# Value products in blocks of four from the first head on, and seven later query products spread over the feed-forward groups

## The chip, the cores and the metric

The kernel runs on one core of a Trainium2 chip. The metric is the device time of one execution in microseconds (us), smaller is better; three runs of the kernel before have a median of 1342.93 us (1341.37 to 1343.72). The profiled execution, whose trace is read here, took 1341.01 us, of which 1338.9 us lie between its first and its last instruction (the span). Differences of under 0.2% (2.7 us) are what a measurement of this kernel cannot tell from no change.

## The reference

With x of 2048 rows and 512 columns, in float32:

```python
q = (x @ wq) in 32 heads of 16; k = x @ wk; v = x @ wv      # one key and value head for all
p = softmax(q k^T / 4);  a = (p @ v, heads side by side) @ wo
b = (silu(x @ w_gate) * (x @ w_up)) @ w_down                # 1792 wide inside
g = sigmoid(sum(x * gate_w));  out = g * a + (1 - g) * b
```

Each head has 2048 x 2048 scores, so exp is taken of 134 million numbers in all.

## The kernel before, in words

Every product outside the value product is made of split operands: a number is a high part (fp32r) and a low part, and three products (high high, high low, low high) are summed. TensorE (PE) is shared by two kinds of work that are woven into one stream by hand (`manual_schedule`: each engine's instructions stand in the order in which the Python code makes them).

**Attention.** A unit u is one head (u // 16) and one block of 128 keys (u % 16). `score(u, j)` (line 669) makes one tile: 128 keys against 1024 queries, two matmuls that each use 64 rows of the array. ScalarE (ACT) takes exp of the tile, from PSUM (two tiles `pss`) to the SBUF tile `pt` (line 684); in some cases VectorE (DVE) first copies half of a tile to SBUF (line 680) and ACT takes exp of that half there. `mix(u)` (line 688) multiplies the exps of a unit with the values and a column of ones, four matmuls in groups of 32 array columns, summed into the PSUM tile `po` over the 16 units of a head. At a head's end `po` is copied to `osb`, inverted, multiplied and stored in DRAM (`o_d`), in small pieces that are handed out over the next units (`LATER`).

**Fillers.** The list `JOBS` holds query products (`query(m, c)`: heads 8m to 8m+7, 512 of the rows), gate and up products of the feed-forward part (`gate_up`) and down products (`down`). A job has 12 or 15 steps; `Halves.step` (line 401) makes one step of one job on the lower 64 rows of the array and one of an older job on the upper 64 rows, side by side. The scores and the fillers use the array in 64-row halves; `mix` uses it in 32-column groups. The gate and up weights of the next columns are loaded by SyncE's (SP's) queue into a raw tile (`wraw`, two buffers) and split on GpSimd (POOL) into a high and a low tile (line 135); `load_w` is called for the first nine weights after the line that loads head 1's queries (lines 781 to 786).

**The order before.** After the keys and values, the four query products of m = 0 run, and three more of m = 1 (`fill(GAP)`, line 648). Then come 16 rounds of two units each (`BEGIN`, lines 790 to 811): four score tiles, eight filler steps, `settle` (what DVE still owes the fillers), and `mix` of two units. In these rounds the other nine query products are the first fillers, and only then the first gate product. One transitional block (`TURN`, line 817) follows, and then blocks of four units (line 821): eight score tiles and 16 filler steps in the order `STEPS`, DVE's half copies for three of eight tiles (`KINDS`), and `mix` of four units in one go. After the last unit the jobs that are left run whole, and then the output product.

**Query products before.** The end of a query product (`keep`, line 224) for m > 0 is five DVE instructions (high part, low part, scaled, absolute bound, largest value) and three stores to DRAM (`q_d`), from which `load_head` fetches each head's queries one head ahead.

Of the kernel before, what the change touches and what calls it, by code (L numbers as in the profile page):

```python
# [46 lines left out]
PTB = 3  # L47
WRB = 2
BLOCK = 4
BEGIN = 16  # L50
STOP = 2
EARLY = 6
OUTS = (1, 2, 3, 0)
# [3 lines left out]
TURN = "SS" + "SFF" * 8  # L57
# [5 lines left out]
def tile_gated_mix(ctx, tc, x, wq, wk, wv, wo, w_gate, w_up, w_down, gate_w, out):  # L63
# [30 lines left out]

    qpool = tc.alloc_tile_pool(name="qpool", bufs=1, side="right")
# [7 lines left out]
    ACC, PAIR = {}, []  # L103
# [19 lines left out]
    ACTS, DEFER, LOADS, HOLD, EVAC, FRESH = [], [], [], [], [], set()  # L123
# [5 lines left out]
    def settle():  # L129
        FRESH.clear()  # L130
        run(ACTS, len(ACTS))
        while DEFER:
            DEFER.pop(0)[2]()
# [77 lines left out]
    def load_wq(m):  # L211
        WQ[m] = load_split(wq_v[:, :, m * P:(m + 1) * P], f"wq{m}", 1, qpool)

    def query(m, c):
# [8 lines left out]

        def keep(ps):
            qh = wp.tile([P, CH], F32R, name="hh", bufs=7)
            ql = wp.tile([P, CH], F32R, name="hl", bufs=7)

            if m:
                qb = wp.tile([P, CH], F32, name="ht" if c % 2 else "hs", bufs=2)
                nc.vector.tensor_copy(qh, ps)  # L230
            else:
                qb = wp.tile([P, CH], F32R, name="hl" if c % 2 else "hh", bufs=7).bitcast(F32)
                nc.scalar.activation(qh, ps, AF.Copy)
                nc.scalar.activation(qb.bitcast(F32R), ps, AF.Abs, scale=kmax)
            nc.vector.tensor_tensor(ql, ps, qh.bitcast(F32), ALU.subtract)
            if m:
                nc.vector.tensor_scalar(qb, qh.bitcast(F32), kmax, None, op0=ALU.mult)
                nc.vector.scalar_tensor_tensor(qb.bitcast(F32R), qb, -1.0, qb, op0=ALU.mult, op1=ALU.max)
# [7 lines left out]
            def store():  # L246
                for j, part in enumerate(parts):
                    nc.sync.dma_start(q_d[m * HG:(m + 1) * HG, j * DH:(j + 1) * DH, cs], part.bitcast(F32))

            if m:  # L250
                store()
            else:
                STORES.append(store)
            nc.vector.tensor_reduce(top[:, t:t + 1], qb, axis=AX.X, op=ALU.max)

        return Job(3 * KD, lambda: m in WQ, terms, keep)

    def queries():
        jobs = [query(m, c) for m in range(1, KD) for c in range(NCH)]
        jobs[-1].after.append(open_acc)  # L260
        jobs[-1].after.append(lambda: nc.vector.tensor_reduce(top[:, KD * NCH:], top[:, :KD * NCH], axis=AX.X, op=ALU.max))
        return jobs

    def open_acc():
        qpool.release()
        for name in ("accp", "bp2"):
            PAIR.append(tc.alloc_tile_pool(name=name, bufs=3, side="right"))
# [60 lines left out]
    def down(ns, c, i):  # L328
# [11 lines left out]
        def add(ps):  # L340
            if c not in ACC:
                ACC[c] = PAIR[0].tile([P, TC, D], F32, name="acc")
# [11 lines left out]


    def jobs():
        late = []
        for m, c in enumerate(ORDER):
            for fs in GROUPS:
# [137 lines left out]
    with tc.tile_pool(name="apool", bufs=1) as ap, tc.tile_pool(name="apool2", bufs=2) as a2:  # L497
# [71 lines left out]
        def project_kv(c):  # L569
            cs = slice(c * CH, (c + 1) * CH)  # L570
            if c % 2 == 0:
                VZ[c // 2] = ap.tile([KW, 2 * CH], F32, name="vz", bufs=2)
# [33 lines left out]
        with tc.manual_schedule():  # L606
# [28 lines left out]
            for c in range(NCH):  # L635
# [5 lines left out]
                if c == 0:  # L641
# [6 lines left out]
            fill(GAP)  # L648

# [3 lines left out]
    with tc.tile_pool(name="bpool", bufs=2) as bp:  # L653
# [11 lines left out]
        def new_pt(u):  # L665
            late = u > PTB * (BEGIN * 2 // PTB) and (u - 2 * BEGIN) % (2 * PTB) >= PTB
            PT[u] = (PAIR[1] if late else bp).tile([P, S], F32, name="pt", bufs=PTB)

        def score(u, j, half=False):
            h, kt = divmod(u, NT)  # L670
            if j == 0:
                new_pt(u)
# [54 lines left out]
        def block(k, first, last, steps, kinds, order):  # L727
# [48 lines left out]
            FRESH.clear()  # L776
            for u in range(BLOCK * k, BLOCK * (k + 1)):
# [9 lines left out]
        with tc.manual_schedule():  # L787
            for j in range(2):
                exps(*score(0, j))
            for n in range(BEGIN):  # L790
                quota = RATE
                u = 2 * n
                if n == 0:
                    feed(FIRST)
                exps(*score(u + 1, 0))
                if n == 0:
                    feed(quota - FIRST)
                exps(*score(u + 1, 1))
                feed(FIRST)
                exps(*score(u + 2, 0))  # L800
                feed(quota - FIRST)
                exps(*score(u + 2, 1))
                settle()
                mix(u)
                mix(u + 1)
                halves.clock += LONG
                run(COPY, 1)
                if LATER:
                    LATER.pop(0)[1]()
                if n == NT // 2 + 1:  # L810
                    load_head(2)
            assert PAIR
            for k in range(2 * BEGIN // BLOCK, NB):
                u = BLOCK * k
                if k == 2 * BEGIN // BLOCK:
                    n = u + 6 - (u + 1)
                    block(k, u + 1, u + 6, TURN, "A" * 2 * n, [f"{i}d" for i in range(2 * n)])
                elif k == NB - 1:
# [13 lines left out]
    PAIR.pop().release()  # L832

    with tc.tile_pool(name="tpool", bufs=2) as tp, tc.tile_pool(name="rpool", bufs=1, side="right") as rp, \
# [3 lines left out]
        ACC[0] = rp.tile([P, TC, D], F32, name="again")  # L838

# [7 lines left out]
        while JOBS:  # L847
            assert JOBS[0].ready()

            if len(JOBS) == TC:  # L850
# [16 lines left out]
    PAIR.pop().release()  # L867
# [78 lines left out]
```

## Time and profile before

| what | value |
|---|---|
| median of three runs | 1342.93 us |
| profiled execution | 1341.01 us, span 1338.9 us |
| PE busy | 1327.0 us (99%) |
| ACT busy | 1061.6 us (79%) |
| DVE busy | 710.1 us (53%) |
| POOL busy | 226.1 us (17%) |
| first score tile starts | 47.94 us |
| first `mix` of the block after the transitional one | 146.87 us |
| `mix` of the last full block | 1251.87 us |

Times in the views are counted from the first instruction. A row of the timeline has start, length, engine, line, operation, `out<-in`, the shape in the array (`64*128` is a half of the rows, `128*32` a group of columns), and in brackets the idle time before it and what ended it. SPq is SP's queue of transfer issues; POOL rows are a little rough. A row of the windows has a stretch and its length, and then the busy time of each engine (with the number of instructions), PEclk, the share in which the transfer engines were busy and what they moved.

### The profile page before, as it was taken

The numbers are of one execution on the slowest core, as the hardware profiler recorded it, in microseconds if no ns is written. First come the engines' busy times: TensorE is split into PE (matmuls) and PEld (weight loads), VectorE is DVE, ScalarE is ACT, GpSimd is POOL, SyncE is SP. The second block draws the span as 40 slices with busy tenths as digits, with TensorE's granted clock in tenths as the row PEclk, the third lists the DMA queues.
The fourth block names the chain that finished last, engine by engine and source line by source line (L and its number), as shares of the span: only waits on it lengthen the run. The fifth ranks groups of instructions, "written<-read, shape, count | busy, mean of one in ns | idle before, by whom it ended". The sixth has DMA issues, their size and how long they took to land. (4 is left out here: it accounts for less than half of the span.)

```text
span 1338.9 us, 26760 instructions
## 1 busy us (share of the span) xinstructions
PE 1327.0 (99%) x10743; PEld 768.8 (57%) x10743; DVE 710.1 (53%) x1221; ACT 1061.6 (79%) x1463; POOL 226.1 (17%) x240
## 2 busy tenths in 40 slices
PE   9999999999999999999999999999999999999998
PEld 7655555555555555555555555555555555555586
DVE  4555565565456565555555556455445555455442
ACT  4578888888888888888888888888888888888500
POOL 6140321152042141143020000000000000001234
PEclk9999999999999999999999999999999999999999
DMA  8455221141234372265162442242122442333254
GB/s 278 139 182 184 66 60 37 36 107 45 59 108 147 121 230 68 68 216 155 46 212 71 135 122 84 68 144 85 56 95 68 134 139 68 99 116 107 63 174 143
DMA packets 104176, 151.83 MB, mean 113 GB/s; under 512 B 12656, under 2 KB 43632, under 8 KB 102384
## 3 DMA queue, kind: packets, MB, share of 16 engines
q1 hardware_dynamic: 102320, 149.86, 36.2%
q8 instruction: 88, 1.44, 0.5%
q10 hardware_dynamic: 1728, 0.20, 0.1%
q14 instruction: 40, 0.33, 0.1%
HBM read 98.11 MB, written 51.38 MB: 112 GB/s over the span
## 5 line engine op out<-in xcount | busy, mean ns | idle before, releaser
L684 ACT ACTIVATE pt<-pss 128x1024 f32<-128x1024 f32 (+1 forms) x1024 | 842.0, 876 | 177.1 <-PE pss L676 145.8
L680 DVE COPY pt<-pss 128x512 f32<-128x512 f32 x354 | 244.9, 692 | 420.9 <-PE pss L676 386.9
L696 PE MATMUL po<-pt,vaug 128*32 128x512 f32 x4096 | 467.6, 595 | 0.0
L676 PE MATMUL pss<-qs,ks 64*128 64x512 f32 x2048 | 402.7, 417 | 1.2 <-ACT pt L684 1.1
L676 PEld LDWEIGHTS pss<-qs,ks 64*128 64x128 f32 x2048 | 193.0, 184 | 219.1 <-ACT pt L684 183.4
L696 PEld LDWEIGHTS po<-pt,vaug 128*32 128x32 f32 x4096 | 119.2, 109 | 260.2 <-issue 255.2
L684 ACT ACTIVATE pt<-pt 128x512 f32<-128x512 f32 x354 | 195.7, 620 | 0.0
L192 PE MATMUL pf<-xh,wgl 64*128 64x512 f32 (+1 forms) x440 | 162.0, 391 | 0.0
L192 PE MATMUL pf<-xh,wgh 64*128 64x512 f32 (+1 forms) x440 | 160.5, 391 | 0.3
L192 PE MATMUL pf<-xl,wgh 64*128 64x512 f32 (+1 forms) x440 | 160.0, 390 | 0.0
L192 PE MATMUL pf<-xh,wuh 64*128 64x512 f32 (+1 forms) x440 | 158.3, 392 | 0.5 <-DVE sign L419 0.3
L192 PE MATMUL pf<-xl,wuh 64*128 64x512 f32 (+1 forms) x440 | 158.3, 390 | 0.0
L192 PE MATMUL pf<-xh,wul 64*128 64x512 f32 (+1 forms) x440 | 157.2, 391 | 0.2 <-POOL wul L108 0.2
L192 PE MATMUL pf<-wdh,hl 64*128 64x512 f32 (+1 forms) x427 | 143.8, 390 | 0.0
L192 PE MATMUL pf<-wdh,hh 64*128 64x512 f32 (+1 forms) x427 | 143.6, 390 | 0.0
L192 PE MATMUL pf<-wdl,hh 64*128 64x512 f32 (+1 forms) x427 | 143.4, 390 | 0.0
L705 DVE RECIPROCAL rsb<-rsb 128x128 f32<-128x128 f32 x128 | 117.1, 935 | 10.0 <-issue 7.8
L107 POOL CAST xh<-wraw 128x512 fp32r<-128x512 f32 x16 | 9.8, 611 | 555.8 <-DMA wraw<-o_d 555.8
L192 PEld LDWEIGHTS pf<-xh,wgh 64*128 64x128 f32 (+1 forms) x440 | 78.5, 185 | 9.1 <-issue 1.8
L192 PEld LDWEIGHTS pf<-xh,wuh 64*128 64x128 f32 (+1 forms) x440 | 77.2, 185 | 9.5 <-issue 1.9
L192 PEld LDWEIGHTS pf<-xl,wgh 64*128 64x128 f32 (+1 forms) x440 | 78.5, 185 | 5.5
L192 PEld LDWEIGHTS pf<-xh,wgl 64*128 64x128 f32 (+1 forms) x440 | 78.5, 185 | 5.3
(157 smaller groups left out, 1351.6 us busy)
## 6 DMA issues: line engine op xcount, KB each, us to landing
qs<-q_d SPq DMA_DIRECT2D x62, 192.0 KB
wraw<-in_B_w_gate_dram SPq DMA_DIRECT2D x28, 256.0 KB
wraw<-in_B_w_up_dram SPq DMA_DIRECT2D x28, 256.0 KB
wraw<-in_B_w_down_dram SPq DMA_DIRECT2D x28, 256.0 KB
wgh<-w_d SPq DMA_DIRECT2D x28, 256.0 KB
wgl<-w_d SPq DMA_DIRECT2D x28, 256.0 KB
wuh<-w_d SPq DMA_DIRECT2D x28, 256.0 KB
wul<-w_d SPq DMA_DIRECT2D x28, 256.0 KB
```

What stands on the lines that cost most here:

```text
L107: eng_hi.tensor_copy(hi, src)
L192: ins = nc.tensor.matmul(self.ps, a, b, start=(i == 0 and not half), stop=(last and half != 0))
L676: nc.tensor.matmul(ps[:, b * CH:(b + 1) * CH], ks[rows, kt * P:(kt + 1) * P], QS[h][rows, j, :], start=True, stop=True)
L680: other = nc.vector.tensor_copy(pt[:, CH:], ps[:, CH:]) if half else None
L684: ins = nc.scalar.activation(pt[:, w], ps[:, w], AF.Exp, scale=SCALE)
L696: nc.tensor.matmul(po[c * 2 * DH:(c + 1) * 2 * DH, :], vaug[:, kt, :], pt[:, c * CH:(c + 1) * CH], start=(kt == 0), stop=(kt == NT - 1))
L705: nc.vector.reciprocal(rsb[:, w], rsb[:, w])
```

## The change

It does four things at once.

1. The rounds of two units and the transitional block go. After an opening of four score tiles and eight filler steps (`OPEN`), all 128 blocks are of four units, with DVE's half copies and `mix` of four units. The six `pt` buffers come from one pool.
2. Of the twelve query products of m = 1 to 3, three run before the first score tile: (1, 2), (1, 3), (2, 3), those that read the upper half of x, which leaves SBUF there. Two, (1, 0) and (1, 1), are the first fillers. The other seven stand one each in the first seven feed-forward groups, after the group's fifth job (`LATE`).
3. A query product's high part, and its bound, are made by ACT for the three early ones (two instructions, as for m = 0). For the other nine DVE makes the high and the low part at once, and scaling, bound and largest value are put off (`DEFER`, or `SOON`, a block later). The seven late ones write to a tile of their own (`qh`) and to one of the two buffers of `osb`.
4. The split query weights, and the raw values `vz`, stand in the three accumulator tiles (`HOME`) until these are needed. `load_wq(3)` comes ahead of the stores of m = 0.

The core of the diff:

```diff
-PTB = 3
+PTB = 6
-BEGIN = 16
+EARLY_Q = ((1, 2), (1, 3), (2, 3))
+SECOND_Q = ((1, 0), (1, 1))
+LATE = {(0, 0): (2, 0), (0, 1): (3, 0), (0, 2): (2, 1), (1, 0): (3, 1), (1, 1): (2, 2), (1, 2): (3, 2), (2, 0): (3, 3)}
-TURN = "SS" + "SFF" * 8
+OPEN = "SFSFFFSFFFSF"
...
+        late = (m, c) in LATE.values()
+        behind = late or (m, c) in SECOND_Q
         def keep(ps):
...
+            if late:
+                qh = hp.tile([P, CH], F32R, name="qh", bufs=1)
+                ql = hp.tile([P, CH], F32, name="osb").bitcast(F32R)
+                qb = qh.bitcast(F32)
...
+            if behind:
                 nc.vector.tensor_copy(qh, ps)
             else:
                 nc.scalar.activation(qh, ps, AF.Copy)
                 nc.scalar.activation(qb.bitcast(F32R), ps, AF.Abs, scale=kmax)
             nc.vector.tensor_tensor(ql, ps, qh.bitcast(F32), ALU.subtract)
...
+            if behind:
+                store([0, 1])
+                (SOON if late else DEFER).extend([((m, c), 0.5, scale), ((m, c), 0.7, bound), ((m, c), 0.7, most)])
...
     def queries():
+        return [query(m, c) for m, c in EARLY_Q + SECOND_Q]
...
                     yield job
                     if late and j:
                         yield late.pop(0)
+                    if j == 4:
+                        if (m, GROUPS.index(fs)) in last:
+                            yield last[m, GROUPS.index(fs)]
...
+            load_wq(3)
             run(STORES, NCH)
-            load_wq(3)
             fill(GAP)
...
         with tc.manual_schedule():
-            for j in range(2):
-                exps(*score(0, j))
-            for n in range(BEGIN):
...
-            for k in range(2 * BEGIN // BLOCK, NB):
+            tiles = [(u, j) for u in range(2) for j in range(2)]
+            for what in OPEN:
+                if what == "S":
+                    exps(*score(*tiles.pop(0)))
+                else:
+                    feed(1)
+            for k in range(NB):
```

How the instructions stand now, at three places. First PE, right after the first value products (`pss` is a score tile, `pf` a filler's PSUM tile; line numbers of the two kernels differ). Before, two score tiles are followed by steps of two query products:

```order
L676 MATMUL pss<-qs,ks 128x512 [waits Activation_49]
L676 MATMUL pss<-qs,ks 128x512
L192 MATMUL pf<-xl,wq2h 128x512
L192 MATMUL pf<-xh_326,wq1h 128x512 [waits DVE_49]
L192 MATMUL pf<-xh,wq2l 128x512
L192 MATMUL pf<-xl_327,wq1h 128x512
```

Now the first gate product begins there, in the 25th filler step (`acc` is a query weight in its new home, `wgh` and `wgl` are the split gate weight):

```order
L704 MATMUL pss<-qs,ks 128x512 [waits Activation_49]
L704 MATMUL pss<-qs,ks 128x512
L198 MATMUL pf<-xh,wgh 128x512 [waits Pool_49]
L198 MATMUL pf<-xl,acc 128x512
L198 MATMUL pf<-xl,wgh 128x512
L198 MATMUL pf<-xh,acc 128x512
L198 MATMUL pf<-xh,wgl 128x512 [waits Pool_49]
```

The first gate product moved from the 109th filler step that PE takes after the first score tile to the 25th, and it waits for POOL's two split halves.

Second SP's queue, where the first gate weight is fetched. Before:

```order
L248 DMA q_d<-hh 8x16x512 [waits DMAHW0_49]
L248 DMA q_d<-hs 8x16x512 [waits DMAHW1_49,DVE_49]
L661 DMA qs<-q_d 16x2x512 [waits DMAHW2_49]
L662 DMA qs<-q_d 48x2x512 [waits DMAHW3_49]
L661 DMA qs<-q_d 16x2x512 [waits DMAHW4_49]
L662 DMA qs<-q_d 48x2x512 [waits DMAHW5_49]
L138 DMA wraw<-in_B_w_gate_dram 128x4x128 [waits DMAHW6_49,Pool_49]
L138 DMA wraw<-in_B_w_up_dram 128x4x128 [waits DMAHW7_49,Pool_49]
```

Now:

```order
L264 DMA q_d<-hh 8x16x512 [waits DMAHW0_49,Activation_49]
L264 DMA q_d<-ht 8x16x512 [waits DMAHW1_49,Activation_49]
L693 DMA qs<-q_d 16x2x512 [waits DMAHW2_49]
L694 DMA qs<-q_d 48x2x512 [waits DMAHW3_49]
L693 DMA qs<-q_d 16x2x512 [waits DMAHW4_49]
L694 DMA qs<-q_d 48x2x512 [waits DMAHW5_49]
L144 DMA wraw<-in_B_w_gate_dram 128x4x128 [waits DMAHW6_49,Pool_49]
L144 DMA wraw<-in_B_w_up_dram 128x4x128 [waits DMAHW7_49,Pool_49]
```

The first gate weight keeps its place in the queue: 26 transfers stand between the last of the `qs` writes of head 0 and it, in both programs the same ones in kind (12 stores of m = 0, nine of three query products, one query weight, four loads of head 1).

Third ACT, around the first exp. Before:

```order
L233 ACTIVATE hh<-pf 128x512 [waits PE_49]
L234 ACTIVATE hl<-pf,kmax 128x512
L684 ACTIVATE pt<-pss 128x1024 [waits DMAHW3_49,DMAHW2_49,DMAHW4_49,DMAHW1_49,DMAHW5_49,DMAHW0_49,DMAHW6_49,PE_49,DMAHW7_49,Activation_49,Pool_49]
L684 ACTIVATE pt<-pss 128x1024 [waits PE_49] x5
L684 ACTIVATE pt<-pss 128x1024 [waits PE_49,Activation_49]
```

Now:

```order
L712 ACTIVATE pt<-pss 128x1024 [waits DMAHW3_49,DMAHW4_49,DMAHW2_49,DMAHW5_49,DMAHW1_49,DMAHW6_49,DMAHW0_49,DMAHW7_49,PE_49,Activation_49]
L252 ACTIVATE hh<-pf 128x512 [waits DMAHW6_49,DMAHW4_49,Activation_49]
L253 ACTIVATE hs<-pf,kmax 128x512
L252 ACTIVATE hh<-pf 128x512 [waits DMAHW7_49,Activation_49]
L253 ACTIVATE ht<-pf,kmax 128x512
L712 ACTIVATE pt<-pss 128x1024 [waits PE_49] x4
```

Between the first exp and the second now stand the ends of two query products, and each writes a tile `hh` whose former content, a part of m = 0's queries, must have been stored first.

More of the change, by code (lines that the diff above doesn't have):

```diff
@@ L341, in add @@
             if c not in ACC:
-                ACC[c] = PAIR[0].tile([P, TC, D], F32, name="acc")
+                assert len(ACC) < 2 or not any(job in JOBS for job in last.values())
+                ACC[c] = accp.tile([P, TC, D], F32, name="acc")
             acc = ACC[c]
@@ L353, in store_acc @@
         nc.sync.dma_start(a_d[c], ACC[c])
+    last = {place: query(m, c) for place, (m, c) in LATE.items()}
     def jobs():
@@ L848, in tile_gated_mix @@
             assert JOBS[0].ready()
-            if len(JOBS) == TC:
+            if len(JOBS) <= TC and OUTS[1] not in OT:
                 load_o(OUTS[1])
```

101 lines of the change are left out of this document (43 added, 58 removed).

## The prediction

> **What bounds the kernel now.** I read the page's busy times first, then PE's timeline, then the windows of the stages, then SP's queue and POOL around the first loads.
>
> ```profile
> PE 1327.0 (99%) x10743; PEld 768.8 (57%) x10743; DVE 710.1 (53%) x1221; ACT 1061.6 (79%) x1463; POOL 226.1 (17%) x240
> L676 PE MATMUL pss<-qs,ks 64*128 64x512 f32 x2048 | 402.7, 417 | 1.2 <-ACT pt L684 1.1
> ```
>
> PE is busy 99% of the span and its scores waited 1.2 us in all. So the end is set by PE's stream: it comes earlier only if PE does the same products in less time, and any new wait of PE counts in full. The change makes the same products (the fillers' steps and the jobs left after the last unit do not change in number), so there are two questions: what a block of four costs against two rounds of two, and whether PE finds its operands ready.
>
> The first is in the windows, cut where a `mix` starts (two scores and eight steps in the third row are 55.22 to 58.25, without the `mix`):
>
> ```profile
> core 0: us, PE busy (x) PEld busy (x) DVE busy (x) ACT busy (x) POOL busy (x), PEclk, DMA share, GB/s
> 47.94:53.37 5.43, 5.43 (x30) 3.94 (x29) 3.60 (x6) 4.36 (x5) 0.00 (x0) 1.00 0.52 182
> 53.37:58.25 4.88, 4.88 (x42) 2.59 (x41) 2.68 (x7) 3.78 (x5) 0.00 (x0) 1.00 0.53 202
> 55.22:58.25 3.03, 3.03 (x29) 2.18 (x25) 0.90 (x3) 2.42 (x3) 0.00 (x0) 1.00 0.53 201
> 126.55:137.39 10.84, 9.89 (x69) 4.59 (x67) 4.32 (x9) 10.30 (x13) 0.00 (x0) 1.00 0.68 179
> 146.87:156.29 9.42, 9.42 (x82) 5.17 (x80) 5.18 (x10) 8.45 (x14) 2.24 (x3) 1.00 0.18 52
> 146.87:1251.87 1105.00, 1103.90 (x9317) 618.00 (x9315) 603.88 (x1037) 957.40 (x1342) 144.92 (x150) 1.00 0.33 101
> ```
>
> A round of two units takes 4.88 us, so 9.76 for four. A block of four takes 9.42 (the mean of the 117 in the last row is 1105.00 / 117 = 9.44). The transitional block takes 10.84 with two more score tiles than a block. PE is counted busy in all of them: the difference lies in the turns between row halves and column groups, not in idle time.
>
> **What the change saves on PE.** Before, from the first score tile (47.94) to the `mix` at 146.87 are 98.93 us, for 84 score tiles, 168 filler steps and the `mix` of 36 units. Now the same work is the opening (four tiles and eight steps, as in the 3.03 us row), nine blocks, and the tiles and steps of a tenth block. Those take 9.42 less its `mix`, which starts at 430.09 and makes way for the next score at 433.66, 3.57 us later:
>
> ```profile
> 430.09 3.64 PE L696 MATMUL po<-pt,vaug 128*32 128x512 f32 x32
> 433.66 0.73 PE L676 MATMUL pss<-qs,ks 64*128 64x512 f32 x4
> 434.23 0.39 PE L192 MATMUL pf<-wdh,hl 64*128 64x512 f32 x1
> 110.41 0.39 PE L192 MATMUL pf<-xh,wgh 64*128 64x512 f32 x1
> ```
>
> So 3.03 + 9 x 9.42 + 5.85 = 93.7 us instead of 98.93: **5.3 us saved**, if nothing is late.
>
> **What is late: the first gate weight.** Before, nine query products fill the rounds, and the first gate product starts at 110.41. Now only two stand ahead of it. It comes after the opening, one block and two score tiles: 47.94 + 3.03 + 9.42 + 0.57 = 60.9 (0.57 is from 433.66 to the first filler step at 434.23). When is its weight there? POOL's and SP's rows:
>
> ```profile
> 43.63 0.77 SPq L248 DMA_DIRECT2D q_d<-hl  x1
> 44.46 1.29 SPq L248 DMA_DIRECT2D q_d<-hh  x2
> 48.74 2.91 SPq L248 DMA_DIRECT2D q_d<-hl  x2
> ...
> 56.76 1.24 SPq L248 DMA_DIRECT2D q_d<-hl  x1
> 58.10 1.14 SPq L138 DMA_DIRECT2D wraw<-in_A_wq_dram  x1
> ...
> 73.58 1.48 SPq L662 DMA_DIRECT2D qs<-q_d  x1
> 75.17 0.52 SPq L138 DMA_DIRECT2D wraw<-in_B_w_gate_dram  x1
> 75.80 0.45 SPq L138 DMA_DIRECT2D wraw<-in_B_w_up_dram  x1
> ...
> 64.45 0.61 POOL L107 CAST wq3h<-wraw 128x512 fp32r<-128x512 f32 x1 [27.70 <-DMA wraw<-in_A_wq_dram]
> 79.14 0.61 POOL L107 CAST wgh<-wraw 128x512 fp32r<-128x512 f32 x1 [12.70 <-DMA wraw<-in_B_w_gate_dram]
> 79.83 1.29 POOL L108 TENSOR_TENSOR wgl<-wraw,wgh 128x512 fp32r<-128x512 f32 x1
> 81.75 1.29 POOL L108 TENSOR_TENSOR wul<-wraw,wuh 128x512 fp32r<-128x512 f32 x1
> ```
>
> SP issues 26 transfers from 43.63 to 75.17, 1.21 us each, back to back, and POOL idles 12.70 us until the raw gate weight lands. In the changed program the same 26 transfers stand ahead of it; only the query weight among them moved to the front. What feeds them is ready in time (the early query products are done on PE by the first score tile). So I take the same times: the high half at 79.75, the low half at 81.12. The first step wants the high half, the third the low half: PE makes two steps (0.46) and waits until about 81.2 for what it would have begun at 61.4, **19.8 us of wait**. Behind that matmul PE's whole stream is queued, scores and `mix` too, so ACT and DVE stand as well. The later weights are in time: the up weight's low half ends at 83.04 and is wanted ten steps and four tiles after 81.2, near 85; the next gate weight is wanted a block later, and the first down weights only after ten gate and up products.
>
> If the transfers ran at the 0.5 us of an issue that finds the queue empty (the two rows at 75), the wait would vanish. If each took the 1.46 us of the slow pair (48.74, 2.91 for two), it would be 26 x 0.25 = 6.5 us longer. The row that is nearest is the same 26 transfers, and I take it.
>
> **The opening.** ACT now ends two query products between its first and second exp, and each writes a tile whose store must have landed. The trace shows that wait where DVE does it before:
>
> ```profile
> 49.67 0.69 DVE L230 CAST hh<-pf 128x512 fp32r<-128x512 f32 x1 [3.81 <-DMA q_d<-hh]
> 37.16 0.60 ACT L233 ACTIVATE hh<-pf 128x512 fp32r<-128x512 f32 x1 [1.54 <-PE pf L192]
> 37.66 0.68 ACT L234 ACTIVATE hh<-pf,kmax 128x512 fp32r<-128x512 f32 x1
> 48.63 3.77 ACT L684 ACTIVATE pt<-pss 128x1024 f32<-128x1024 f32 x4 [7.57 <-issue]
> ```
>
> The store lands at 49.67, or some 1.2 us later with the query weight ahead of it. Then come 0.60 + 0.68 twice, so the second exp starts near 53.4 instead of 49.6. PE's fourth score tile needs that exp's PSUM: about 3.9 us of wait. It costs nothing, since PE then waits for the gate weight anyway (60.9 becomes 64.8, before 79.75). Were the weight in time, it would cost 3.9.
>
> **After the gap.** PE will have stood some 15 us. Its longest gap so far is 1.17 us, after which the rate is about the same (four transposes take 0.66 us against 0.61). But the first matmuls of the trace are slow: thirty from 0.99 to 4.16, 106 ns each, then six from 4.61 to 4.94, 55 ns each, though PEclk shows 1.00 there.
>
> ```profile
> 0.99 3.33 PE L545 MATMUL po<-warm 128*128 128x128 bf16 x30 [0.99 <-DVE warm L609]
> 4.16 0.61 PE L558 MATMUL pss<-ident,xt 128*128 128x128 f32 x4
> 4.61 0.50 PE L545 MATMUL po<-warm 128*128 128x128 bf16 x6
> 4.94 0.61 PE L558 MATMUL pss<-ident,xt 128*128 128x128 f32 x4
> 8.11 0.66 PE L558 MATMUL pss<-ident,xt 128*128 128x128 f32 x4 [1.17 <-DMA xt<-in_A_x_dram]
> ```
>
> A 15 us gap is nearer to that start than to 1.17 us, so I take half speed for 3.2 us once more, 1.6 us lost; the bounds are 0 and 1.6. The Trainium skill, "TensorE: Matmul & The Clock Gate" (Part 1: The HAM clock gate), says that the array drops to half its clock after about 3.4 us without work and needs about 3.4 us of work to come back; by it the loss would be about 1.7 us, and no run here yet shows the drop after a gap.
>
> **The seven late query products.** PE's share only moves. On DVE each is a high part, a low part, a scaling, a bound and a maximum, as in the rounds before:
>
> ```profile
> 43.33 0.69 DVE L235 TENSOR_TENSOR hl<-pf,hh 128x512 fp32r<-128x512 f32 x1
> 43.94 0.48 DVE L237 TENSOR_SCALAR hs<-hh,kmax 128x512 f32<-128x512 f32 x1
> 44.45 0.69 DVE L238 SCALAR_TENSOR_TENSOR hs<-hs 128x512 fp32r<-128x512 f32 x1
> 45.18 0.69 DVE L254 TENSOR_REDUCE top<-hs 128x1 f32<-128x512 f32 x1
> ```
>
> That is 4 x 0.69 + 0.48 = 3.24 us, spread over two or three blocks in which DVE is busy 5.18 of 9.42. The idle 4.2 us of each block hide it; without that cover the 1.38 us of the first two would delay a half copy, and with it a score tile. The scaling waits for a store issued a block (9 us) earlier; landing took 5 us in the row at 49.67 (issued at 44.46). The late products' buffer of `osb` is free since the head before. Bounds: 0 and 7 x 1.38 = 9.7; I take 1 us, near zero, because the idle time exceeds the need threefold. Queue entries (21 stores) only move.
>
> **Sum.** +19.8 - 5.3 + 1.6 + 1.0 = +17.1 us on the profiled execution's 1341.01, so 1358.1. The median of the runs is 1.92 above that execution: 1342.93 + 17.1 = **1360 us**. Its own range, from the bounds without the empty-queue case, is 1342.93 + 19.8 - 5.3 - 3 = 1354 (loads 3 us earlier, no clock loss, no late cost) to 1342.93 + 17.1 + 6.5 = 1367.
>
> **Rivals.** (a) *The weight is in time.* If PE's early stores drained at the empty-queue rate, the gate weight would be split by 61. For it speak the 0.5 us issues; against it, that 26 transfers in a row kept 1.21 us. Then the opening's 3.9 us show: 1342.93 - 5.3 + 3.9 + 1.0 = 1342.5, no change. It decides from the point where the low half is there before 61.4 + 3.9. (b) *In time, and the opening does not wait either* (the stores land early too): 1338.6, faster. (c) *The late products cost what they need.* Each delays PE by 1.38 us and its `osb` copy holds the next head's DVE work for about as much: 7 x 2.8 = 19.3, so 1360 + 18 = 1378. Against it stands DVE's idle time.
>
> **How the numbers follow.** Forecast 0.86, (a) 0.05, (b) 0.04, (c) 0.05. Faster by over 0.2% (2.7 us, what a measurement can tell) is (b), 0.04; within it (a), 0.06 with the edge of the forecast; slower is the forecast and (c), 0.90. The range 1350 to 1367 holds the forecast's own and some milder cases; (a), (b) and (c) lie outside.
>
> **What would show it.** In the changed profile PE should stand once, from about 65 to 79.8, released by POOL's gate weight, with rows of 0.39 us steps doubled for about 3 us behind it; SP should issue the first gate weight near 75; ACT's second exp should start near 53. Then blocks of 9.4 us, the tenth `mix` near 163 instead of 146.87, and blocks with a late query product no longer than the others. An issue of the gate weight before 60, or a PE without a gap, would make the forecast wrong.

## The result, and the profile after

The changed kernel takes 1372.09 us (median of six runs, 1370.84 to 1373.55) against 1342.78 us for the kernel before on the same chip (six runs, 1341.37 to 1344.01): a ratio of 1.0219, 95% interval 1.0208 to 1.0229. It is slower by 29.3 us where 17.1 were forecast. The profiled execution took 1372.81 us, its span is 1371.0 us, 32.1 more than before.

The page, the same two rows as those shown of before:

```profile
PE 1335.2 (97%) x10743; PEld 775.5 (57%) x10743; DVE 726.0 (53%) x1239; ACT 1069.0 (78%) x1496; POOL 227.5 (17%) x240
L704 PE MATMUL pss<-qs,ks 64*128 64x512 f32 x2048 | 405.0, 418 | 3.7 <-ACT pt L712 3.6
```

PE's busy time grew by 8.2 us (1327.0 to 1335.2) although it makes the same products, and the span by 32.1. So PE stood some 24 us longer, and some of its matmuls were slower. The windows say where (columns as in those of before: length; busy PE, PEld, DVE, ACT, POOL; PEclk). The rows are: the opening from the first score tile to the first `mix`; the first block; the blocks up to the tenth `mix`; the blocks to the `mix` of the last full one; the tail.

```profile
48.14:64.94 16.80, 13.36 (x56) 9.19 (x56) 4.76 (x9) 11.46 (x16) 0.70 (x1) 0.70 0.52 194
64.94:87.44 22.50, 11.47 (x82) 6.26 (x80) 4.37 (x8) 8.06 (x12) 6.63 (x8) 0.77 0.54 161
87.44:163.26 75.82, 75.72 (x642) 42.92 (x640) 46.66 (x79) 65.64 (x93) 28.90 (x29) 1.00 0.38 100
163.26:1283.53 1120.27, 1109.32 (x9318) 618.89 (x9316) 617.31 (x1056) 956.06 (x1339) 134.59 (x138) 1.00 0.34 102
1283.53:1371.00 87.47, 80.34 (x387) 60.51 (x385) 29.37 (x46) 7.92 (x11) 32.09 (x34) 0.98 0.45 145
```

The tenth `mix` starts at 163.26 (forecast "near 163"; the same work ended at 146.87 before): +16.4 us. The stretch behind it takes 1120.27 instead of 1105.00: **+15.3 us, where 1.0 was forecast**. The tail takes 87.47 instead of 1338.9 - 1251.87 = 87.03: +0.4. The sum is 32.1.

**The early part** is the forecast's, step by step. The timelines of ACT, PE, SP and POOL:

```profile
53.15 1.94 ACT L712 ACTIVATE pt<-pss 128x1024 f32<-128x1024 f32 x2
...
54.23 0.80 PE L704 MATMUL pss<-qs,ks 64*128 64x512 f32 x2 [3.20 <-ACT pt L712]
...
74.84 0.52 SPq L144 DMA_DIRECT2D wraw<-in_B_w_gate_dram  x1
...
79.47 0.61 POOL L111 CAST wgh<-wraw 128x512 fp32r<-128x512 f32 x1 [30.62 <-DMA wraw<-in_B_w_gate_dram]
80.16 1.28 POOL L112 TENSOR_TENSOR wgl<-wraw,wgh 128x512 fp32r<-128x512 f32 x1
...
80.13 0.79 PE L198 MATMUL pf<-xh,wgh 64*128 64x512 f32 x1 [10.90 <-POOL wgh L111]
84.02 0.39 PE L198 MATMUL pf<-xh,wgh 64*128 64x512 f32 x1
```

ACT's second exp starts at 53.15 (forecast 53.4), SP issues the first gate weight at 74.84 (75), POOL's halves end at 80.08 and 81.44 (79.75 and 81.12), and PE's steps are slow until 84.0. Behind the wait the eight blocks up to the tenth `mix` take 75.82 us, against 8 x 9.42 = 75.4, so the price of a block held too. One thing here was not forecast: PE also ran at half clock in the opening, behind its 3.20 us wait, so the first `mix` came at 64.94 and not near 60.7. The gate weight's wait was shorter by as much, 10.90 us, and its end did not move.

**The later part** has waits for up weights that the kernel before does not have. Those for `wuh`, the split up weight's high half (us in total, times, longest):

```profile
PE pf L198 <- POOL wuh L111: 3.8, 2, 2.4
...
PE pf L198 <- DMA wuh<-w_d: 2.4, 1, 2.4
```

They lie in the blocks that start at 468.74, 584.74 and 703.51. These take 11.70, 14.07 and 12.58 us, and the one behind the third 10.63; over 9.42 each that is 11.3 us. The largest is the block from 584.74 to 598.81. SP's queue, POOL and PE there; `w_d` is the DRAM copy of the split weights that the second quarter of x writes for the later ones:

```profile
575.00 0.66 SPq L264 DMA_DIRECT2D q_d<-osb  x1
576.41 0.56 SPq L144 DMA_DIRECT2D wraw<-in_B_w_down_dram  x1
577.08 1.22 SPq L166 DMA_DIRECT2D w_d<-wdh  x1
...
578.81 1.60 SPq L144 DMA_DIRECT2D wraw<-in_B_w_down_dram  x1
582.83 0.32 SPq L166 DMA_DIRECT2D w_d<-wdh  x1
...
588.00 0.58 SPq L144 DMA_DIRECT2D wraw<-in_B_w_down_dram  x1
...
589.58 0.50 SPq L144 DMA_DIRECT2D wraw<-in_B_w_up_dram  x1
...
593.88 0.61 POOL L111 CAST wuh<-wraw 128x512 fp32r<-128x512 f32 x1
...
594.54 0.50 PE L198 MATMUL pf<-xh,wuh 64*128 64x512 f32 x1 [2.41 <-POOL wuh L111]
```

A late query product has just ended (the first row is one of its two stores there). Behind them SP issues down weights, and between them stores to `w_d` that wait until POOL has split the weight. The next up weight is issued only at 589.58, as the fourth weight behind the query product's two stores (three down weights and the four loads of the next head's queries go first); PE wants it at 594.54 - 2.41 = 592.13 and gets it at 594.49. After the wait PE is slow again (steps start 0.43 us apart instead of 0.23).

In the kernel before, three rows of SP's queue in the same quarter of x are these; left out between the first and the second are two more down weights and stores to `w_d`:

```profile
581.02 0.48 SPq L138 DMA_DIRECT2D wraw<-in_B_w_gate_dram  x1
...
590.35 0.46 SPq L138 DMA_DIRECT2D wraw<-in_B_w_down_dram  x1
...
594.10 0.39 SPq L138 DMA_DIRECT2D wraw<-in_B_w_up_dram  x1
```

There at most three down weights stand between a gate weight and the next up weight in this quarter, at the three places of the changed kernel four or five. The late products outside the second quarter of x cost no such wait. In the first quarter four or five down weights go ahead of the up weight as well (from 221 to 262 us and from 337 to 375), but without stores to `w_d` between them, and PE does not wait.

### The profile page after: what moved, and what is told of

The parts are those of the page before. It is cut to its first block, busy times and chain, and to the rows that moved or that the text cites. A ratio compares the mean times of both kernels' runs of the same rounds, so it can differ in the third digit from the quotient of the medians.

```text
span 1371.0 us, 26854 instructions
## 1 busy us (share of the span) xinstructions
PE 1335.2 (97%) x10743; PEld 775.5 (57%) x10743; DVE 726.0 (53%) x1239; ACT 1069.0 (78%) x1496; POOL 227.5 (17%) x240
## 5 line engine op out<-in xcount | busy, mean ns | idle before, releaser
L712 ACT ACTIVATE pt<-pss 128x1024 f32<-128x1024 f32 (+1 forms) x1024 | 832.5, 864 | 198.4 <-PE pss L704 169.4
L708 DVE COPY pt<-pss 128x512 f32<-128x512 f32 x381 | 263.3, 691 | 470.8 <-PE pss L704 433.4
L704 PEld LDWEIGHTS pss<-qs,ks 64*128 64x128 f32 x2048 | 195.9, 185 | 214.2 <-ACT pt L712 172.1
L712 ACT ACTIVATE pt<-pt 128x512 f32<-128x512 f32 x381 | 210.7, 620 | 0.1
L198 PE MATMUL pf<-xh,wgh 64*128 64x512 f32 (+1 forms) x440 | 164.4, 394 | 14.4 <-POOL wgh L111 10.9
L198 PE MATMUL pf<-xh,wuh 64*128 64x512 f32 (+1 forms) x440 | 161.9, 394 | 6.3 <-POOL wuh L111 3.8
L198 PE MATMUL pf<-xl,wgh 64*128 64x512 f32 (+1 forms) x440 | 163.6, 392 | 0.0
L198 PE MATMUL pf<-xh,wul 64*128 64x512 f32 (+1 forms) x440 | 161.9, 394 | 0.9 <-POOL wul L112 0.9
L198 PE MATMUL pf<-xl,wuh 64*128 64x512 f32 (+1 forms) x440 | 161.3, 392 | 0.0
L198 PEld LDWEIGHTS pf<-xh,wgh 64*128 64x128 f32 (+1 forms) x440 | 80.0, 185 | 25.1 <-POOL wgh L111 11.3
L198 PEld LDWEIGHTS pf<-xh,wul 64*128 64x128 f32 (+1 forms) x440 | 79.4, 185 | 7.6 <-POOL wul L112 1.7
```

The source lines that it names most:

```text
L198: ins = nc.tensor.matmul(self.ps, a, b, start=(i == 0 and not half), stop=(last and half != 0))
L704: nc.tensor.matmul(ps[:, b * CH:(b + 1) * CH], ks[rows, kt * P:(kt + 1) * P], QS[h][rows, j, :], start=True, stop=True)
L708: other = nc.vector.tensor_copy(pt[:, CH:], ps[:, CH:]) if half else None
L712: ins = nc.scalar.activation(pt[:, w], ps[:, w], AF.Exp, scale=SCALE)
```

## The experiments

The question was where the 15.3 us of the later part come from, and whether the early wait is what it was taken for. All runs are compared by medians and by the windows of their profiled execution; where an expectation speaks of the second or fifth run, the runs are counted in the order given here. "Rest" is from the tenth `mix` to the `mix` of the last full block; all kernels make the same work there (before: 1105.00; in e7 with twelve steps in the opening it lies four steps later in the same list).

| kernel | ratio to before (95%) | first `mix` | tenth `mix` | rest | span |
|---|---|---|---|---|---|
| changed | 1.0219 (1.0208 to 1.0229) | 64.94 | 163.26 | 1120.27 | 1371.0 |
| e1 | 1.0183 (1.0162 to 1.0203) | 64.09 | 159.25 | 1120.50 | 1367.4 |
| e2 | 1.0151 (1.0130 to 1.0172) | 64.64 | 163.01 | 1109.10 | 1359.4 |
| e3 | 1.0143 (1.0122 to 1.0165) | 64.35 | 163.96 | 1108.62 | 1360.3 |
| e5 | 1.0100 (1.0081 to 1.0118) | 62.37 | 158.86 | 1109.33 | 1355.3 |
| e6 | 1.0055 (1.0041 to 1.0068) | 64.43 | 150.91 | 1107.62 | 1345.8 |
| e7 | 1.0090 (1.0076 to 1.0104) | 59.40 | 153.88 | 1109.36 | 1352.2 |
| e8 | 1.0088 (1.0074 to 1.0102) | 60.30 | 155.38 | 1108.75 | 1351.3 |
| e9 | 1.0010 (1.0001 to 1.0019) | 61.59 | 147.80 | 1108.24 | 1343.3 |
| e10 | 1.0013 (1.0003 to 1.0023) | 58.89 | 145.78 | 1108.23 | 1341.1 |

**e1: the gate weight ahead of the stores.** The first gate and up weights are loaded ahead of the stores of m = 0 and of `load_head(1)`.

```diff
             load_wq(3)
+            load_w("g", 0)
             run(STORES, NCH)
+            load_w("u", 0)
+            load_w("g", 1)
+            load_w("u", 1)
             fill(GAP)
...
-        for n in range(2):
-            load_w("g", n)
-            load_w("u", n)
```

> The changed kernel with one edit: the first two gate and up weights are fetched earlier (the first ahead of the stores of m = 0, the other three ahead of the three early query products' stores). Theory 1 (PE stood because 26 transfers are ahead of that weight in the queue): the second block falls from 22.50 to about 9.5 us, so 1372.1 - 13 = 1359 us (1356 to 1362). The opening stays slow or gets up to 1.2 us slower. Rival (the transfers' rate is the limit and the wait only moves, to the next weights or to the first scores): 1366 or more, with a new gap of PE before 110 us. The stalls near blocks 42, 54 and 66 stay by both.

Measured: 1368.54 us, 3.6 less. The first block takes 10.06 us instead of 22.50, so the wait at 69 to 80 us was the order in SP's queue. But as the rival had it, a wait came back three blocks later. SP, POOL and PE there:

```profile
88.31 6.83 SPq L144 DMA_DIRECT2D wraw<-in_B_w_down_dram  x3
97.18 0.38 SPq L144 DMA_DIRECT2D wraw<-in_B_w_gate_dram  x1
...
103.30 0.61 POOL L111 CAST wgh<-wraw 128x512 fp32r<-128x512 f32 x1 [3.91 <-DMA wraw<-in_B_w_gate_dram]
...
103.96 0.80 PE L198 MATMUL pf<-xh,wgh 64*128 64x512 f32 x2 [6.17 <-POOL wgh L111]
```

PE reaches the third gate product 12 us earlier than before the edit, while its weight stands behind five down weights that SP can issue only as POOL empties the two raw buffers, and behind query stores. That block takes 18.71 us, 9.3 too many. The wait was not a single late weight but a stage in which SP and POOL have more to do than PE's work ahead covers.

**e2 and e3: the late product's place, and the loads that its end sets off.** Every product's end issues up to two loads from a list; the list is filled with the next group's down weights when the last down product ends, and in the changed kernel a late query product ends right behind that. e2 puts the late product one job later, behind the group's sixth job:

```diff
-                    if j == 4:
+                    if j == 5:
```

> The changed kernel with one edit: each late query product stands after the sixth job of its group (an up product) instead of the fifth. Theory 2 (the stalls at blocks 42, 54 and 66 come from the order in SP's queue: with the late product right behind the last down product, two more down weights and their copies to DRAM pass ahead of the next up weight): these stalls go, 12 us less, 1360 us (1358 to 1364), and PE does not wait for an up weight. Rival (the 3.24 us of DVE work of each late product delay PE, wherever it stands): 1369 to 1375.

e3 leaves it in its place and only keeps its end from issuing loads:

```diff
+            self.loads = True
...
-                run(LOADS, 2)
+                if self.loads:
+                    run(LOADS, 2)
...
+    for job in last.values():
+        job.loads = False
```

> The changed kernel with one edit: the end of a late query product issues no down weights, these wait for the next job's end. The late products and their stores stay where they were. Theory 2 (order of the weight loads): 1360 to 1364 us, no wait for an up weight. Rival 2b (the two stores of the late product block the queue or take its bandwidth, whatever order the loads have): 1369 to 1374 us, PE still waits for up weights in the second quarter of x.

Measured: 1363.15 and 1362.93 us, 8.9 and 9.2 less by the medians. In the profiled executions, of which there is one each, the rest falls by 11.2 and 11.7 us, the same by both edits, and as much as the four long blocks had lost (11.3). The waits of e2 and of e3, by what PE waited for (us in total, times, longest):

```profile
PE pf L198 <- POOL wgh L111: 10.8, 1, 10.8
...
PE pf L198 <- DVE sign L447: 1.9, 3, 0.9
...
PE pf L198 <- DVE ht L332: 0.9, 1, 0.9
```

```profile
PE pf L199 <- POOL wgh L111: 11.2, 1, 11.2
...
PE pf L199 <- DVE sign L451: 2.2, 3, 1.6
...
PE pf L199 <- DVE ht L334: 0.9, 1, 0.9
```

No row for `wuh` is left, neither from POOL nor from DRAM. Since e3 keeps the late products' stores and their place, these stores are not the cause; the order of the loads is. (At the second of the three places e3 still has four down weights ahead of the up weight, in place of five; it is issued at 585.68 instead of 589.58, and that is enough.) What remains in both is DVE: about 2.8 to 3.1 us of waits.

**e5: e1 and e2 together, and the first query product of m = 0 stored at its end** (so that ACT's first tile is free earlier).

```diff
                 STORES.append(store)
+                if c == 0:
+                    run(STORES, 1)
```

> The changed kernel with three edits: the early gate and up weights of e1, the late products after the sixth job as in e2, and the stores of the first query product of m = 0 issued at its end, so that ACT need not wait for them in the opening. If the three causes are the whole loss: the opening up to the first value product takes 9 to 10 us instead of 17.0, the second block 9.4, and no up weight is late: 1372.1 - 13 - 12 - 8 = 1339 us (1336 to 1342), 3 to 5 us less than the kernel before, by the 5.3 us that blocks of four save. Rival (what the blocks save is lost again to DVE, which now has half copies and feed-forward work in the first blocks): 1343 to 1348.

Measured: 1356.84 us, 18 more than expected. Three things were missed. The wait for the third gate weight is there as in e1 (4.35 us; that block takes 16.38 us). The second block takes 13.86 us: the scaling that was put off starts in DVE's stream only when an earlier store of its tile has landed,

```profile
77.20 0.49 DVE L267 TENSOR_SCALAR ht<-hh,kmax 128x512 f32<-128x512 f32 x1 [6.32 <-DMA q_d<-ht]
```

and the half copy behind it comes late, so that a score tile of PE waits 1.94 us and the clock is at 0.72 for the next 6 us. And from the first tile to the first `mix` are 13.71 us, where 9 to 10 were expected (16.80 in the changed kernel), though ACT's wait is gone. The windows of its opening:

```profile
50.00:54.00 4.00, 2.76 (x14) 1.44 (x13) 0.49 (x1) 4.00 (x5) 3.42 (x4) 1.00 0.60 184
54.00:58.00 4.00, 4.00 (x15) 3.15 (x15) 2.15 (x5) 1.99 (x4) 0.32 (x1) 0.51 0.52 202
```

PE's timeline in the first of them:

```profile
50.96 0.50 PE L710 MATMUL pss<-qs,ks 64*128 64x512 f32 x2 [0.64 <-ACT pt L718]
52.80 0.50 PE L710 MATMUL pss<-qs,ks 64*128 64x512 f32 x2 [0.18 <-ACT pt L718]
53.71 0.51 PE L710 MATMUL pss<-qs,ks 64*128 64x512 f32 x2 [0.41 <-ACT pt L718]
```

Three short waits, and from about 54 on the clock is halved all the same. So it takes no single long wait to lose the clock.

**e6: six query products ahead of the first gate product** instead of two (SECOND_Q also holds (2, 0), (3, 0), (2, 1), (3, 1)); the three that are left come behind the sixth job, as in e2.

```diff
-SECOND_Q = ((1, 0), (1, 1))
-LATE = {(0, 0): (2, 0), (0, 1): (3, 0), (0, 2): (2, 1), (1, 0): (3, 1), (1, 1): (2, 2), (1, 2): (3, 2), (2, 0): (3, 3)}
+SECOND_Q = ((1, 0), (1, 1), (2, 0), (3, 0), (2, 1), (3, 1))
+LATE = {(1, 1): (2, 2), (1, 2): (3, 2), (2, 0): (3, 3)}
...
-                    if j == 4:
+                    if j == 5:
```

> The changed kernel with four of the seven late query products (those of the x quarters 0 and 1) put back in the row ahead of the first gate product, so that six stand there instead of two, and the three that are left yielded behind the fourth up product as in the second run. The first gate weight is still issued near 75 us. Theory (the gap at 69 to 80 us is the missing cover, and the late products themselves cost next to nothing): the first gate product is now wanted near 120 us, the gap goes and does not move elsewhere; from the span of the second run, 1359.4, go 13.0 + 0.5: about 1346, median about 1348. The opening's 16.7 us (8.9 at full clock) stay. Rival: the six products have to end on VectorE into tiles whose stores stand in SP's queue behind the weight loads, PE waits for their PSUM instead, 5 us or more between 65 and 130 us: 1353 or more.

Measured: 1349.0 us, as the theory had it (1348). The windows of its opening and of the nine blocks behind it:

```profile
48.00:64.43 16.43, 12.92 (x55) 8.87 (x56) 4.76 (x9) 11.41 (x16) 0.56 (x1) 0.69 0.52 197
64.43:150.91 86.48, 86.08 (x721) 48.12 (x719) 54.84 (x95) 73.24 (x104) 29.13 (x30) 1.00 0.49 147
```

The nine blocks take 86.48 us (9 x 9.42 = 84.8) with PE busy in all but 0.4: the wait is gone and did not move elsewhere. So the early query products were the cover for the first gate weights, and four more of them are enough (fewer were not tried). The opening is now the one large loss (16.4 us instead of the 8.9 of the sum).

**e7: e6 with a fed opening.** The first store at its product's end as in e5, and twelve filler steps instead of eight between the four opening tiles.

```diff
-OPEN = "SFSFFFSFFFSF"
+OPEN = "SFFSFFFFSFFFFSFF"
```

> As the run before, and the opening changed in two ways: the store of the first early query product is issued at that product's end (as in the fourth run), and twelve filler steps instead of eight stand between the four opening score tiles. Theory (the clock falls because PE stands idle in the opening, and the filler steps cover ScalarE's late exps): the first mix of four comes near 58 (the opening's 3.0 us plus 0.9 for four more steps plus the 5.85 of a block's tiles and steps, from 48.1) instead of 64.6, and the median is about 6 to 7 us below the run before, near 1341: no slower than the kernel before. Rival (PE waits for ScalarE's exps all the same, and even gaps below 1 us, as in the fourth run, are followed by the half clock): first mix at 62 or later, 2 us or less gained.

Measured: 1354.23 us, 5 more than e6 instead of 7 less, though its opening did what was expected: first `mix` at 59.40, PE's waits 0.42 us, the clock at 1.00 throughout. Two of its stretches:

```profile
50.00:54.00 4.00, 3.41 (x18) 2.15 (x18) 1.28 (x3) 4.00 (x6) 1.88 (x2) 1.00 0.50 165
...
108.47:125.04 16.57, 11.17 (x82) 5.68 (x80) 8.09 (x14) 9.80 (x16) 4.15 (x4) 0.94 0.59 185
```

SP, POOL and PE in the second:

```profile
98.50 0.61 SPq L264 DMA_DIRECT2D q_d<-hl  x1
...
115.93 0.53 SPq L144 DMA_DIRECT2D wraw<-in_B_w_gate_dram  x1
...
120.59 1.04 POOL L111 CAST wgh<-wraw 128x512 fp32r<-128x512 f32 x1 [17.82 <-DMA wraw<-in_B_w_gate_dram]
...
121.69 0.50 PE L198 MATMUL pf<-xh,wgh 64*128 64x512 f32 x2 [3.40 <-POOL wgh L111]
```

PE now wants the third gate weight at 121.69 - 3.40 = 118.29, 8.6 us earlier than e6's PE took it (126.88): 5 by the opening, the rest by the four steps, which put it ahead of a `mix` (3.6 us) instead of behind it. It is issued at 115.93, behind eleven query stores and the four loads of head 2's queries, which SP could begin at 98.50 only, when the last down weight had its raw buffer. The wait is 3.40 us and the block takes 7.2 us too many, with shorter waits for ACT (1.37) and for the low half (0.62). In e6 the slow opening had hidden that. The tail takes 1.7 us more (88.96): four steps earlier, the last up product ends right ahead of the down product that needs it, and PE waits 1.89 us for DVE.

**e8: e5 with the down weights in turn.** The second up weight and the first five down weights go to the list, two at each product's end, instead of standing ahead of the first product.

```diff
-            load_w("u", 1)
...
-        for n in GROUPS[0]:
-            load_w("d", n)
+        LOADS.append(lambda: load_w("u", 1))
+        LOADS.extend([lambda n=n: load_w("d", n) for n in GROUPS[0]])
```

> The fourth run (gate weight early, late product behind the fourth up product, early store) with the second up weight and the first five down weights put into the list from which two loads are issued at each product's end, instead of all ahead of the first product; so the third gate weight, issued at the end of the first gate product, has at most four loads ahead of it. Theory (the 4.35 us wait at 103.9 us in the fourth run is the third gate weight behind five down weights in SP's queue): block 4 takes 9.5 instead of 16.4; the median falls from 1356.8 to about 1350 (and to 1346 if the 1.9 us wait at 79.9, VectorE behind a store's landing, goes too). Rival (the early transfers are limited by what the DMA queues move, so any order leaves a gap of this size somewhere before 130 us): 1355 or more.

Measured: 1353.66 us, between the two expectations. The kernel before was 1.1 us faster in these runs than in e5's, and the ratios of e5 and e8 have intervals that overlap, so the timed runs do not separate the two. In the profiled executions the gap is still there: the block from 89.70 takes 18.47 us (16.38 in e5), with 3.58 us for the third gate weight at 97.59 and 1.81 for its up weight. With two query products ahead, PE reaches the weights sooner than SP and POOL bring them, in both of the orders tried. What the profile shows as gained on e5 is the second block (9.93 instead of 13.86) and the opening (2 us), in which the clock stayed up this time.

**e9: e6 with the first five down weights behind the second up product,** the early store of e5, and the loads of the late products' ends held as in e3.

```diff
+        if n == 1:
+            r[1].after.append(lambda: LOADS.extend([lambda d=d: load_w("d", d) for d in GROUPS[0]]))
...
-        for n in GROUPS[0]:
-            load_w("d", n)
```

> As the fifth run (six query products ahead of the first gate product, three late ones behind the fourth up product), and: the first early query product is stored at its end; the first five down weights are put on the list at the end of the second up product instead of ahead of everything; the end of a late query product issues no load from the list. The opening keeps its eight filler steps. Theory: the opening is shortened as in the fourth and seventh run (first mix 60.3 to 62.4 instead of 64.4), SP no longer stands from 85 to 98 us for POOL's splits of the down weights, so the third gate weight is issued some 10 us earlier and is in time although PE comes earlier; median 1349.0 less 2 to 4: 1345 to 1347. Rival (the fifteen stores of the six products, 1.2 us each, hold the third gate weight wherever the down weights stand): PE waits 2 us or more for it between 115 and 130 us, median 1350 or more.

**e10: e9 with four filler steps moved from the first block to the opening,** so that everything behind is the same.

```diff
-OPEN = "SFSFFFSFFFSF"
+OPEN = "SFFSFFFFSFFFFSFF"
+STEPS0 = "SSFFFFSFSFFSFFSFFFSS"
...
-                    block(k, u + 2, u + 6, STEPS, KINDS, EXPS)
+                    block(k, u + 2, u + 6, STEPS if k else STEPS0, KINDS, EXPS)
```

> As the run before, with twelve filler steps in the opening instead of eight and twelve instead of sixteen in the first block, so that all later blocks and the tail hold the same steps as there. Theory (steps instead of waits in the opening keep the clock up, as in the sixth run): first mix near 58.5 to 59.4 instead of 60.3 to 62.4, median 1342 to 1344, which is within 0.2% of the kernel before or just above: all that the change adds is gone but not more, since of the 5.3 us that blocks of four save the opening (first mix 53.4 before) takes 5 back. Rival (a block of twelve steps is set by ScalarE's exps): the second mix comes 9.4 us or more after the first and nothing is gained on the run before.

Measured: 1345.19 and 1344.37 us against 1342.64 for before (21 runs). In e9 SP issues the third gate weight at 108.16 instead of 117.60 in e6, and PE does not wait for it although it comes earlier. In e10 the first `mix` comes at 58.89 as expected, but the timed runs of the two do not differ (the intervals overlap), and the median lies just above the 1342 to 1344 expected. With the change's waits mended, some 0.1% is left of the 2.2%, and nothing is gained on the kernel before. The windows of e10:

```profile
48.00:58.89 10.89, 10.11 (x58) 6.71 (x56) 3.85 (x8) 9.78 (x14) 1.90 (x2) 1.00 0.53 180
58.89:145.78 86.89, 86.03 (x722) 47.90 (x720) 55.41 (x95) 73.41 (x104) 25.58 (x26) 1.00 0.47 149
```

From the first tile to the tenth `mix` are 97.78 us, against 98.93 before: the blocks of four do save, but 1.2 us and not 5.3. Of the 4.1 that are missing, 2.0 stand in the opening (10.89 against 8.88), where ACT still ends two query products between its first exps and PE stands 0.78 us, and 2.1 in the nine blocks (86.89 against 84.78), where it stands 0.86; what the other 2.5 are was not looked into. In the rest, 3.2 us are lost, up to 2.7 of them in PE's waits for DVE in a few blocks (below).

## Why the prediction was right and wrong

- **What bounds the kernel** held: PE is still the bound (97% busy), and each new wait of PE counted in full.
- **The first gate weight, +19.8; blocks of four, -5.3; the clock, +1.6:** together +16.1 were forecast up to the tenth `mix` and +16.4 measured. The mechanism of the wait was shown by taking its cause away in two ways: loading the weight earlier (e1) removed the wait at that place, and putting query products ahead of it again (e6) removed it for good. The drain of SP's queue was right to 0.3 us (74.84 against 75.17).
- **The sizes inside that sum** are less exact than the sum. The clock term was taken for the long wait alone, and was right there: the window from 80.13 to 84.13 has PEclk 0.54, which is 4 x 0.46 = 1.8 us. It was also lost in the opening, some 4 us; the text had the 3.9 us wait there (3.20 measured) but not the slow matmuls behind it. Neither this wait nor these slow matmuls cost anything, because "PE then waits for the gate weight anyway"; e6, where that cover is gone, shows the price, a first `mix` at 64.4 instead of e10's 58.9. The 5.3 us saved are, in the best version, 1.2 at most as a net gain; in the changed kernel the same work ended where it did because the weight's arrival set it. That the sum came out to 0.3 us is in part luck. A row was misread as well: in the transitional block PE is busy 9.89 of 10.84 us and not in all of it, so some 0.95 of the 5.3 us is idle time and not turns.
- **"The later weights are in time"** was right in the changed kernel (the block behind the wait took 9.9 us), because PE had waited: in e1, e5, e7 and e8 the third gate weight is the next one late.
- **The seven late query products, +1.0: this is the step that failed.** The part measured +15.3. DVE's share was weighed, and PE's, and of SP it said "Queue entries (21 stores) only move". Not weighed was that a product's end sets off two loads from the list, so that a late product pulls down weights, and in the second quarter of x the `w_d` stores that wait for POOL between them, ahead of the next up weight. Three of the seven products cost this. e2 and e3 put it at about 9 us by the medians and at 11.2 to 11.7 in the profiled executions, with the late products' own stores cleared by e3. SP's order would have shown it: the up weight stands behind four or five down weights where at most three had stood.
- The remaining 3.6 to 4.1 us of that part lie within the bounds given (0 to 9.7), above the value taken. They are mostly DVE's (2.8 to 3.1 us of PE's waits): with seven late products the rest takes 1109.1 us (e2), with three 1107.6 (e6), before 1105.0. Not all of it is the late products' own work: in e6 a block loses 1.2 us at 264 us, ahead of any late product, so part may be that the fillers now meet the blocks at another phase. How much is the one and how much the other was not settled.
- **Rival (c)** (the late products cost what DVE needs, 1378) came nearest in time and was wrong in kind: it was SP's order, not DVE. Rivals (a) and (b) fell with the wait.
- **The range** (1350 to 1367) was built around the bounds of the early terms; the upper bound of the late products (9.7 us, for DVE alone) was left out of its top. With it the top would have been some 1376, and the result would have lain inside for a wrong reason.

## What to carry to other kernels

Where a product's end issues transfers from a list, a product that is put into the order is also one more turn of that list: look at what the queue issues two places behind the insertion, and at which of those entries wait for another engine. A wait at one weight may be a shortage of the whole stage; bringing that weight forward moved the wait to the next (e1, e5, e8), and more covering work took it away (e6). Where PE came earlier still, the wait was back (e7), and it stayed away with the transfers that are not urgent put behind the urgent ones (e9, e10). And a wait that is hidden behind another should be priced as if it stood alone: the opening's cost nothing here and 5.5 us as soon as the other was mended.

## What was not expected of the hardware

**The clock falls without a long wait.** In the changed kernel PE ran at half clock behind a wait of 3.20 us, and for some 3 us behind one of 2.41 us at 594.54 with 0.47 more at 595.96; behind 1.41 and 0.40 us (476.78 and 478.14) it stayed at 1.00. In the openings of e5 and e9 it fell behind waits of at most 0.64 us. The windows of e9 and e8, the opening of each:

```profile
50.00:54.00 4.00, 3.10 (x13) 1.99 (x14) 0.96 (x2) 4.00 (x6) 1.89 (x2) 0.85 0.48 150
54.00:58.00 4.00, 4.00 (x15) 3.16 (x15) 1.67 (x4) 1.77 (x3) 0.00 (x0) 0.50 0.53 203
```

```profile
50.00:54.00 4.00, 3.05 (x16) 1.60 (x14) 0.00 (x0) 4.00 (x6) 2.44 (x4) 1.00 0.73 205
54.00:58.00 4.00, 3.26 (x20) 2.46 (x19) 2.49 (x5) 2.54 (x4) 1.28 (x1) 1.00 0.51 180
```

PE is busy 3.1 of 4 us in both, and one lost its clock for over 4 us and the other did not; with 3.4 of 4 (e7, e10) neither did. Each is one execution, so this gives no threshold. The Trainium skill, "TensorE: Matmul & The Clock Gate" (Part 1: The HAM clock gate), has the gate look at activity in a free-running window of about 3.4 us, and the array go cold after an idle one; the drop behind 3.20 us comes near that figure, and those behind 2.41 and 0.64 us lie well under it, so a single idle stretch of that length is not what they had in common.

**DVE is held up by POOL's splits.** A DVE instruction and the POOL instruction at the same time, in the changed kernel:

```profile
169.70 1.64 DVE L322 SCALAR_TENSOR_TENSOR ht<-ht,hs 128x512 f32<-128x512 f32 x1
...
169.48 1.30 POOL L112 TENSOR_TENSOR wul<-wraw,wuh 128x512 fp32r<-128x512 f32 x1
```

By the timeline's rows from 140 to 1240 us, this DVE instruction takes 0.68 us on average when no POOL instruction overlaps it by more than 0.1 us (34 rows) and 1.33 when one does (7 rows, up to 1.75); the copies of a score tile from PSUM take 0.69 either way (286 and 59 rows). The stretched one ends about one free duration after POOL's (169.48 + 1.30 + 0.69 = 171.47 against 171.34), as if it had waited for it. This block lost 1.2 us by it. The Trainium skill, "SBUF — State Buffer" (SBUF: two separate sides), says that a DVE instruction with two SBUF inputs and a GpSimd one that reads SBUF exclude each other for their whole length; these rows agree.
